# Six feature tiles transposed in place, and the PSUM banks of the last stage divided three and five

## The chip, the cores and the metric

The kernel runs on one core of one Trainium2 chip. The metric is the device time of one execution in microseconds (us). A core has five engines with an instruction stream each: TensorE (PE, matmul; its weight loads are listed as PEld), VectorE (DVE), ScalarE (ACT), GpSimd (POOL) and SyncE (SP). In this kernel SP issues most DMA transfers and POOL the rest. Each engine executes its stream in order and waits for others by semaphores.

## The reference

Two mixers read one layer norm of the same input, and their results are added to it.

```python
xn = layernorm(x)                                  # x: 1 x 2048 x 512
# A: linear attention, 32 heads of 16, learned softmax features
q, k, v = split_heads(xn @ wqkv)
pq, pk = q @ w_phi, k @ w_phi                      # per head
phi_q = concat(softmax(pq), softmax(-pq))          # phi_k alike, 32 features a head
kv, z = phi_k^T v, sum_s phi_k
o = (phi_q @ kv) / (phi_q . z + 1e-6)
A = merge_heads(o) @ wo                            # 512 x 512
# B: gated MLP with a spatial matmul
h = gelu(xn @ w_in)                                # 2048 x 1376
z1, z2 = h[:, :688], layernorm(h[:, 688:])
g = w_sp @ z2 + b_sp                               # w_sp: 2048 x 2048
B = (z1 * g) @ w_out                               # 688 x 512
out = x + A + B
```

All is float32, to float32 accuracy.

## The kernel before

The 2048 rows are 16 tiles of 128, numbered `s` or `i` from 0 to 15. For accuracy a matmul operand is split into a rounded part `h` (type float32r) and a rest `l`, and one product becomes three matmuls, `h*h`, `h*l` and `l*h` (`mm3`, lines 55 to 57). The first stages project, build the key sums and run the spatial matmul as seven block products per pair of tiles (`products`, `drain`). The unnormalised query features of each tile go to DRAM as `e_d`, and the gated rows `u = z1 * g` as `u_d` and `uT_d`.

This case is about the last stage, which for each pair of tiles (i, i+1) does on PE, in this order:

- `attend_T(i)`: 16 transposes of 128x128 of the pair's query features into four PSUM tiles (`ptq`). ACT copies them out as `f` (line 900).
- `project_u(i)`: 17 matmuls of 512 columns, u times w_out, into the PSUM tile `pout`.
- `attend`: 32 small matmuls (line 912) of `f` with the key-value sums `kvT` into two PSUM tiles `po`. ACT rounds each into `oT` high (line 47), DVE computes the rest (line 51).
- `project_u(i+1)`, 17 matmuls into a second `pout`.
- `project_o` for both tiles: 12 matmuls each, oT times wo, added into the same two `pout`. DVE then adds x (line 944, tile `xr`), and SP stores the result (line 945, `out<-xr`).

Beside this the features of later tiles are made ready (`features(s)`, three tiles ahead): SP loads `et` from `e_d` (line 487), DVE runs seven operations on it (`q_fin`, lines 494 to 501; line 501 writes the finished tile), and POOL issues a DMA that copies `et` into `er` (line 872). That copy gives the tile the type float32r, and the transposes read `er` at line 898. A tile without copy is read at line 896 as float32. Tiles 0 and 1 come from DRAM as float32r, and tiles 2 and 3 have no copy, so 12 tiles have one. The gated rows of later tiles are loaded as `ut`, joined by ACT (line 774) and split by ACT and DVE into `uh`, `ul` and `rt`.

PSUM has eight banks, and each of these tiles fills one. Before, `pst` holds four for `ptq`, and `pso` two for `pout` and two for `po`. A PSUM tile's next use waits until its last reader is done: a `pout` bank is free when DVE has added x from it. The last stage takes over banks in which the seven products of the stage before still stand until `drain` (lines 712 to 717) has read them.

One more piece of the stage before ends here: the gate of the last pair of rows (`gate`, from line 727) is issued in the round i = 8 and needs `z1t`, which `load_z1` fetches with a memset and two DMAs on POOL.

The scheduler orders each engine's stream when the program is built, from its own estimates; `tc.issue_after` pins a few places.

Of the kernel before, what the change touches and what calls it, by code (L numbers as in the profile page):

```python
# [10 lines left out]
F32 = mybir.dt.float32  # L11
# [8 lines left out]
P = 128  # L20
S, D, H, DH, FH = 2048, 512, 32, 16, 688
# [12 lines left out]
NP = NT // 2  # L34
# [5 lines left out]
def mixer(ctx: ExitStack, tc: tile.TileContext, x, x_t, wv, wqkT, phi_bd, wo, w_in, wst, b_r, w_out, out):  # L40
    nc = tc.nc
    pe, act, dve, pool, sp = nc.tensor, nc.scalar, nc.vector, nc.gpsimd, nc.sync


    def round_h(eng, h, src):
        if eng is act:
            return act.activation(h, src, AF.Copy).ins  # L47
        return eng.tensor_copy(h, src).ins

    def rest_l(l, src, h, eng=None):  # L50
        return (eng or dve).tensor_tensor(l, src, h.bitcast(F32), op=ALU.subtract).ins  # L51

    def mm3(dst, a, b, start, stop):
        (ah, al), (bh, bl) = a, b
        pe.matmul(dst, ah, bh, start=start, stop=False)  # L55
        pe.matmul(dst, ah, bl, start=False, stop=False)  # L56
        return pe.matmul(dst, al, bh, start=False, stop=stop).ins  # L57

    def pool_of(name, bufs, side=None, space=None):
        kw = {"space": space} if space else {"side": side}  # L60
        return tc.tile_pool(name=name, bufs=bufs, reuse_waits="tile", **kw)
# [3 lines left out]
    psum = lambda name, bufs: pool_of(name, bufs, space=PSUM)  # L65
# [424 lines left out]
    def q_fin(et, tmp, zb):  # L490

        e, r, t, w = et[:, :NF], *(et[:, NF + k * 2 * H:NF + (k + 1) * 2 * H] for k in range(3))
        den = et[:, NF + 6 * H:QW]
        dve.tensor_tensor(tmp, e, zb, op=ALU.mult)
        dve.tensor_reduce(t, heads(tmp), axis=AX.X, op=ALU.add)
        dve.tensor_tensor(t, t, r, op=ALU.mult)
        dve.scalar_tensor_tensor(den, pairs(t, 0), EPS_DEN, pairs(t, 1), op0=ALU.add, op1=ALU.add)
        dve.reciprocal(den, den)
        dve.tensor_tensor(w.rearrange("p (h a) -> p h a", a=2), r.rearrange("p (h a) -> p h a", a=2),
                          den.unsqueeze(2).to_broadcast([P, H, 2]), op=ALU.mult)  # L500
        return e, dve.tensor_tensor(heads(e), heads(e), bc(w, 2 * H), op=ALU.mult).ins
# [46 lines left out]
    with ExitStack() as p1:  # L548
# [41 lines left out]
        for s in range(NE):  # L590
            et = load_q(s, tb.tile([P, QW], F32, tag="et", bufs=2, name="et"))
            tmp = zw.tile([P, 4, FC], F32, tag="z2", bufs=2, name="qtmp").rearrange("p a b -> p (a b)")[:, :NF]
            e, _ = q_fin(et, tmp, zb)
# [56 lines left out]
    for s in range(NT):  # L650
# [4 lines left out]
        z = z2[n][:, 2 * (s % 2):2 * (s % 2) + 2]  # L655
# [34 lines left out]
    def load_z1(i):  # L690
        t = gt.tile([P, 2, UP], F32, tag="z1", name="z1t")
        pool.memset(t[:, :, FH + REM:], 0.0)
        for k in range(2):
            pool.dma_start(t[:, k, :FH], z1_d[2 * i + k])
        return t
# [46 lines left out]
    def slot(name, dt=F32):  # L742
        return xz.tile([P, 2, FH], dt, tag="xz", name=name).rearrange("p a b -> p (a b)")
# [8 lines left out]
    def split_w(t, h, l):  # L752
        return round_h(act, h, t), rest_l(l, t, h)
# [56 lines left out]
    g, es, ets = {}, {}, {}  # L810
    for n in range(NC):
        i = SEQ[n][0]
        if n % NQ == 1 and i < NP - 1:
            z = load_z1(i)
# [49 lines left out]
    def features(s):  # L864
        with tc.issue_after(fin[-1]):
            es[s], ins = q_fin(ets.pop(s), slot("qtmp")[:, :NF], zb)
        fin.append(ins)
        if s == 3:
            return
        e = es[s]  # L870
        es[s] = cw.tile([P, NF], F32R, tag="er", bufs=5, name="er")
        pool.dma_start(es[s].bitcast(F32), e)

    def gated(t):
        u = joined(t, cw.tile([P, UP], F32, tag="uj", bufs=2, name="uj"))
        return gate_parts(u, wk.tile([P, KF * P], F32R, tag="uh", name="uh"),
                          wk.tile([P, KF * P], F32R, tag="ul", name="ul"), wk.tile([2 * REM, P], F32R, tag="rt", name="rt"))
# [3 lines left out]
    ctx_psg.__exit__(None, None, None)  # L881
    fin.append(last)
    sp.dma_start(kvT.rearrange("p j b -> p (j b)"), kvT_d)
    pst = ctx.enter_context(psum("pst", 4))
    pso = ctx.enter_context(psum("pso", 1))

    def attend_T(s):

        fs = []
        for g in range(NG):  # L890
            pt = pst.tile([P, 2, 2, P], F32, tag="tr", name="ptq")
            for a in range(2):
                for k in range(2):
                    src = group(es[s + k], 2 * g + a)
                    if src.dtype == F32:
                        pe.transpose(pt[:, a, k], src, ident)
                    else:
                        pe.transpose(pt[:, a, k].bitcast(F32R), src, ident_r)  # L898
            f = wk.tile([P, 2, 2 * P], F32, tag="f", bufs=NG + 1, name="f")
            attend_T.last = act.activation(f, pt.rearrange("p a k b -> p a (k b)"), AF.Copy).ins  # L900
            fs.append(f)
        return fs

    def attend(fs):

        oT = [wk.tile([P, NG, 2 * P], F32R, tag=f"oT{k}", name="oT") for k in "hl"]
        po = [pso.tile([P, 2, 2 * P], F32, tag="po", bufs=2, name="po") for _ in range(2)]
        for j in range(2 * NG):
            c = j % NG
            for r in range(2):  # L910
                rows = slice(r * HP, (r + 1) * HP)
                lasts[3] = pe.matmul(po[r][c * QP:(c + 1) * QP, j // NG], kvT[rows, j], fs[j // 2][rows, j % 2],
                                     start=True, stop=True).ins
        for k in range(2):
            gs = slice(2 * k, 2 * k + 2)
            lasts[5] = round_h(act, oT[0][:, gs], po[k])
            ins = rest_l(oT[1][:, gs], po[k], oT[0][:, gs])
        return oT, ins

    def project_u(i, u, between=None):  # L920
        uh, ul, rt = u
        parts = [(slice(0, D), pso.tile([P, D], F32, tag="out", bufs=2, name="pout"))]
        if i == NT - 1:
            more = pst.tile([P, 4, P], F32, tag="tr", name="pout2").rearrange("p a b -> p (a b)")
            parts = [(slice(k * D // 2, (k + 1) * D // 2), q[:, :D // 2]) for k, q in enumerate((parts[0][1], more))]
        order = ExitStack()
        for ds, p in parts:
            for c in range(KF):
                i_ = mm3(p, (uh[:, c], ul[:, c]), tuple(w[:, ds] for w in wu[c]), c == 0, False)
                if between and c == KF // 2:  # L930
                    order.enter_context(between(i_))
            for w in wu[KF]:
                lasts[2] = pe.matmul(p, rt, w[:, ds], start=False, stop=False).ins
        order.close()
        return parts

    def project_o(i, oT, parts):
        ts = slice(i % 2 * P, (i % 2 + 1) * P)
        xr = wk.tile([P, D], F32, tag="xr", bufs=3, name="xr")
        sp.dma_start(xr, x[i * P:(i + 1) * P, :])  # L940
        for ds, p in parts:
            for c in range(ND):
                lasts[4] = mm3(p, (oT[0][:, c, ts], oT[1][:, c, ts]), (wo_h[:, c, ds], wo_l[:, c, ds]), False, c == ND - 1)
            dve.tensor_tensor(xr[:, ds], p, xr[:, ds], op=ALU.add)
            sp.dma_start(out[i * P:(i + 1) * P, ds], xr[:, ds])

    GATE_LAST = 8

    wo_h, wo_l = (cw.tile([P, ND, D], F32R, name=f"wo{k}") for k in "hl")
    p = {0: project_u(0, uT.pop(0))}  # L950
# [4 lines left out]
    with tc.issue_after(attend_T.last):  # L955
        for c in range(ND // 2, ND):
            wo_last, _ = split_w(wo_raw[c], wo_h[:, c], wo_l[:, c])
# [13 lines left out]
    def ahead(i):  # L971

        if 3 < i + 3 < NT:
            features(i + 3)
        if i + 4 < NT:
            ets[i + 4] = load_q(i + 4, slot("et"))
            us[i + 4] = fetch_u(i + 4)

    nxt = {}
    for i in range(0, NT, 2):  # L980
        if i:
            p[i] = project_u(i, nxt.pop(i))
            with tc.issue_after(lasts[2]):
                oT, _ = attend(fT)
            with tc.issue_after(lasts[3]):
                p[i + 1] = project_u(i + 1, nxt.pop(i + 1))
        if i + 2 < NT:
            with tc.issue_after(lasts[5]), tc.issue_after(wo_last):
                nxt[i + 2], nxt[i + 3] = gated(us.pop(i + 2)), gated(us.pop(i + 3))
        for k in range(2):  # L990
            project_o(i + k, oT, p.pop(i + k))
            ahead(i + k)
        if i == GATE_LAST - 4:
            z = load_z1(NP - 1)
        if i == GATE_LAST:
            with tc.issue_after(lasts[0]), tc.issue_after(lasts[1]):
                gate(NP - 1, cb, z, gt.tile([P, 2 * UP], F32, tag="pl", name="pl"))
            p2.close()
        if i + 2 < NT:
            with tc.issue_after(lasts[4]):  # L1000
                fT = attend_T(i + 2)
# [33 lines left out]
```

## Time and profile before

| | |
|---|---|
| time, 3 runs | 634.63 us median (634.57 to 634.85) |
| the profiled execution | 635.8 us, of which 634.1 us are the span from its first to its last instruction |
| granted TensorE clock, mean | 0.997 |
| busy share of the span: PE, DVE, ACT, POOL | 98%, 80%, 50%, 19% |
| the last stage | 493.97 to 634.1 us, 140.1 us |

The times in the views are microseconds from the first instruction of the profiled execution. A row of the timeline has start, duration, engine, line, operation, result and operands, and, in brackets, how long the engine was idle before it and whose signal ended the wait. A PE row's duration reaches beyond the start of the next, since matmuls are pipelined: two starts give the pace. A row of the windows gives the busy time of PE, PEld, DVE, ACT and POOL in a stretch, then the granted clock, the share of the DMA engines' time and GB/s.

### The profile page before, as it was taken

To read this page: it belongs to the slowest core of one execution; us is meant where nothing else is said; L and a number is where in the kernel's file an instruction comes from. 1 tells how busy PE (TensorE), PEld (TensorE's weight loads), DVE (VectorE), ACT (ScalarE), POOL (GpSimd) and SP (SyncE) were. 2 spreads that over 40 slices of the span, in tenths; PEclk is the share of its full clock that TensorE was granted. 3 is DMA by queue.
4 is the path that set the end of the run, shared out by engine and by line. 5 is a ranking of instruction groups with operands and counts; after the bars stand their busy time and mean duration, and the time that the engine had idled before them with its cause. 6 is when DMAs were issued, how large, how long until landed. Compare 5 with 4: busy or idle time off the path is not lost.

```text
span 634.1 us, 11506 instructions
## 1 busy us (share of the span) xinstructions
PE 623.6 (98%) x4375; PEld 563.9 (89%) x4375; DVE 507.1 (80%) x925; ACT 314.5 (50%) x463; POOL 122.3 (19%) x215
## 2 busy tenths in 40 slices
PE   8999999999999999999999999999999998998997
PEld 6888888888888999999999999999999876777776
DVE  5979989998898579889968777688686897999621
ACT  5623333332433447887465444654448552556650
POOL 4542231322101006442011010110103000000100
PEclk9999999999999999999999999999999998999999
DMA  8467676656644941002486776768677968598811
GB/s 329 150 167 161 188 185 147 194 141 155 178 141 108 296 159 67 2 1 68 145 224 173 212 196 177 227 184 228 188 231 255 314 230 279 198 229 307 249 66 36
DMA packets 67379, 113.90 MB, mean 180 GB/s; under 512 B 30620, under 2 KB 32156, under 8 KB 67324
## 3 DMA queue, kind: packets, MB, share of 16 engines
q1 hardware_dynamic: 53036, 63.35, 34.2%
q0 software_dynamic: 11696, 43.65, 24.2%
q10 hardware_dynamic: 2592, 6.16, 2.6%
q8 instruction: 34, 0.56, 0.4%
q14 instruction: 21, 0.17, 0.1%
HBM read 60.69 MB, written 31.48 MB: 145 GB/s over the span
## 4 chain that ended last, share of the span: by engine, by line
PE 82%; DMA 8%; DVE 6%; ACT 2%; issue 2%; SPq 0%; POOL 0%; ACTq 0%; DVEq 0%; POOLq 0%
PE g L57 10%; PE g L56 10%; PE g L55 10%; PE proj L55 6%; PE zps L55 6%; PE proj L57 6%; PE proj L56 6%; PE zps L57 6%; PE zps L56 6%; PE pout L55 3%; PE pout L56 3%; PE pout L57 3%; DMA et<-e_d 2%; DMA eq<-e_d 2%; PE kvps L322 1%
## 5 line engine op out<-in xcount | busy, mean ns | idle before, releaser
L55 PE MATMUL g<-B,A 128*128 128x344 f32 x448 | 143.2, 320 | 0.0
L56 PE MATMUL g<-B,A 128*128 128x344 f32 x448 | 143.2, 320 | 0.0
L57 PE MATMUL g<-B,A 128*128 128x344 f32 x448 | 142.9, 320 | 0.0
L55 PEld LDWEIGHTS g<-B,A 128*128 128x128 f32 x448 | 84.2, 188 | 0.0
L56 PEld LDWEIGHTS g<-B,A 128*128 128x128 f32 x448 | 84.2, 188 | 0.0
L57 PEld LDWEIGHTS g<-B,A 128*128 128x128 f32 x448 | 84.1, 188 | 0.0
L47 ACT ACTIVATE A<-S 128x512 fp32r<-128x512 f32 x64 | 39.7, 629 | 53.7 <-DVE S L538 23.3
L116 ACT ACTIVATE e<-e,r_x 128x1024 f32<-128x1024 f32 x32 | 36.7, 1149 | 46.0 <-DVE e L115 44.2
L51 DVE TENSOR_TENSOR A<-S,A 128x512 fp32r<-128x512 f32 x64 | 43.4, 688 | 17.0 <-ACT A L47 16.7
L55 PE MATMUL proj<-wqk_h,xT 128*128 128x512 f32 x124 | 49.6, 400 | 0.0
L57 PE MATMUL proj<-wqk_h,xT 128*128 128x512 f32 x124 | 48.8, 394 | 0.0
L56 PE MATMUL proj<-wqk_l,xT 128*128 128x512 f32 x124 | 48.7, 393 | 0.0
L118 DVE TENSOR_REDUCE sm<-e 128x64 f32<-128x1024 f32 x32 | 38.6, 1212 | 9.7 <-ACT e L116 9.4
L47 ACT ACTIVATE A<-wf 128x512 fp32r<-128x512 f32 x64 | 33.2, 518 | 26.4 <-PE g L57 20.6
L51 DVE TENSOR_TENSOR A<-wf,A 128x512 fp32r<-128x512 f32 x64 | 35.4, 553 | 9.9 <-ACT A L47 9.5
L55 PE MATMUL zps<-w_h,xT 128*128 128x344 f32 x128 | 41.8, 326 | 0.4 <-ACT z1f L146 0.3
L57 PE MATMUL zps<-w_h,xT 128*128 128x344 f32 x128 | 40.9, 319 | 0.0
L56 PE MATMUL zps<-w_l,xT 128*128 128x344 f32 x128 | 40.8, 319 | 0.0
L146 ACT ACTIVATE z1f<-zps,r_x 128x344 f32<-128x344 f32 (+1 forms) x30 | 17.0, 566 | 33.8 <-PE zps L57 33.3
L302 ACT ACTIVATE v<-proj,r_x 128x512 f32<-128x512 f32 x16 | 11.0, 687 | 44.2 <-PE proj L57 41.7
L55 PE MATMUL pout<-wu,uh 128*128 128x512 f32 (+1 forms) x75 | 30.2, 402 | 2.3 <-DVE rh L734 1.8
L900 ACT ACTIVATE f<-ptq 128x512 f32<-128x512 f32 x32 | 16.5, 601 | 29.4 <-PE ptq L898 23.2
(199 smaller groups left out, 1534.8 us busy)
## 6 DMA issues: line engine op xcount, KB each, us to landing
wf<-in_wst SPq DMA_DIRECT2D x64, 256.0 KB, 3.7
e_d<-e POOLq DMA_DIRECT2D x16, 544.0 KB, 3.7
et<-e_d SPq DMA_DIRECT2D x16, 544.0 KB, 5.1
zacc<-e POOLq DMA_DIRECT2D x16, 512.0 KB, 4.9
er<-et POOLq DMA_DIRECT2D x12, 512.0 KB, 5.3
z_d<-z1f ACTq DMA_DIRECT2D x16, 344.0 KB, 3.8
z1t<-z_d POOLq DMA_DIRECT2D x16, 344.0 KB, 5.7
u_d<-c POOLq DMA_DIRECT2D x14, 384.0 KB, 2.7
```

The costliest lines, as they stand in the source:

```text
L47: return act.activation(h, src, AF.Copy).ins
L51: return (eng or dve).tensor_tensor(l, src, h.bitcast(F32), op=ALU.subtract).ins
L55: pe.matmul(dst, ah, bh, start=start, stop=False)
L56: pe.matmul(dst, ah, bl, start=False, stop=False)
L57: return pe.matmul(dst, al, bh, start=False, stop=stop).ins
L116: softmax_pair.exp = act.activation(e, e, AF.Exp, scale=scale).ins
L118: dve.tensor_reduce(sm, heads(e), axis=AX.X, op=ALU.add)
L146: z1_raw.last = act.activation(z[:, k], p, AF.Copy, scale=r_x[:, s:s + 1]).ins
L302: ins = act.activation(v[s], proj(s, wv_h, wv_l, rest_last), AF.Copy, scale=r_x[:, s:s + 1]).ins
L322: ins = pe.matmul(kv_acc[k:k + QP, m // 4], vs[:, m * QP:(m + 1) * QP], e[:, m * HP:(m + 1) * HP], start=s == 0 and m < 4, stop=s == NT - ...
L900: attend_T.last = act.activation(f, pt.rearrange("p a k b -> p a (k b)"), AF.Copy).ins
```

## The change

Three things change. Features of tiles below `PLAIN = 6` get no copy, so tiles 4 and 5 lose theirs and their transposes read float32. The PSUM pools become five banks for `ptq`, `po` and the odd tile `pout2`, and three for `pout`. And `load_z1(NP - 1)` has to follow the last copy issued before it.

```diff
     def features(s):
...
         fin.append(ins)
-        if s == 3:
+        if s < PLAIN:
             return
         e = es[s]
         es[s] = cw.tile([P, NF], F32R, tag="er", bufs=5, name="er")
-        pool.dma_start(es[s].bitcast(F32), e)
+        features.copied = pool.dma_start(es[s].bitcast(F32), e).ins
...
-    pst = ctx.enter_context(psum("pst", 4))
-    pso = ctx.enter_context(psum("pso", 1))
+    pst = ctx.enter_context(psum("pst", 5))
+    pso = ctx.enter_context(psum("pso", 3))
...
     def attend(fs):
...
-        po = [pso.tile([P, 2, 2 * P], F32, tag="po", bufs=2, name="po") for _ in range(2)]
+        po = [pst.tile([P, 2, 2 * P], F32, tag="tr", name="po") for _ in range(2)]
...
     def project_u(i, u, between=None):
         uh, ul, rt = u
-        parts = [(slice(0, D), pso.tile([P, D], F32, tag="out", bufs=2, name="pout"))]
+        parts = [(slice(0, D), pso.tile([P, D], F32, tag="out", name="pout"))]
...
-    GATE_LAST = 8
+    GATE_LAST, PLAIN = 8, 6
...
         if i == GATE_LAST - 4:
-            z = load_z1(NP - 1)
+            with tc.issue_after(features.copied):
+                z = load_z1(NP - 1)
```

The first place is PE at the transposes of tiles 4 and 5, with - for before and + for the change. `zb` is the slot that holds the float32r identity, `ident` the float32 one.

```order
 L56 MATMUL pout<-wol,oT 128x512
 L57 MATMUL pout<-woh,oT 128x512
-L898 MATMUL ptq<-zb,er 128x128 x16
+L896 MATMUL ptq<-ident,et 128x128 x16
 L55 MATMUL pout<-wu,uh 128x512
 L56 MATMUL pout<-wu,uh 128x512
```

Nothing moved here: the 16 transposes keep their place and read `et`, the tile that DVE writes.

The second place is SP late in the stage, around the load of the last feature tile, number 15 (the first `et` row after the + line), the stores of output tiles 8 and 9 (`out<-xr`) and the loads of x.

```order
 L756 DMA_TRANSPOSE ut<-u_d 128x12x128
+L945 DMA out<-xr 128x512 x2
 L487 DMA et<-e_d 128x1088
-L945 DMA out<-xr 128x512 x2
 L940 DMA xr<-in_x 128x512 x2
 L756 DMA_TRANSPOSE ut<-u_d 128x12x128 x2
```

The load of tile 15 now stands behind the two stores, which wait for DVE's additions; before it stood ahead of them.

The third place is DVE in the same round, where it works on tile 15 (lines 494 and 495) and on the rests of `oT` for the pair (10, 11). Before:

```order
L494 TENSOR_TENSOR qtmp<-et,zb 128x1024
L495 TENSOR_REDUCE et<-qtmp 128x64
L51 TENSOR_TENSOR oT<-po,oT 128x512
L496 TENSOR_TENSOR et<-et 128x64
L51 TENSOR_TENSOR oT<-po,oT 128x512
```

And in the change:

```order
L494 TENSOR_TENSOR qtmp<-et,zb 128x1024
L51 TENSOR_TENSOR oT<-po,oT 128x512 x2
L495 TENSOR_REDUCE et<-qtmp 128x64
L51 TENSOR_TENSOR ul<-uj,uh 128x640
L496 TENSOR_TENSOR et<-et 128x64
```

Both rests moved up by one or two rows, and line 494 of tile 15, the first to need its load, stands ahead of them in both programs.

On POOL the memset and the two loads of `z1t` stand behind the third remaining copy, that of tile 8; before they stood ahead of all copies.

## The prediction

> **What bounds the kernel now.** I read the page first, then windows cut at the start of each pair's transposes in the last stage, then PE's timeline there.
>
> ```profile
> span 634.1 us, 11506 instructions
> PE 623.6 (98%) x4375; PEld 563.9 (89%) x4375; DVE 507.1 (80%) x925; ACT 314.5 (50%) x463; POOL 122.3 (19%) x215
> ```
>
> PE is busy for 623.6 of 634.1 us, so only its gaps and its slow stretches are to be had. The windows show where these lie; the first is pair (0, 1), and so on to (14, 15):
>
> ```profile
> 493.97:510.28 16.31, 16.31 (x109) 12.69 (x108) 13.95 (x22) 10.33 (x16) 0.00 (x0) 1.00 0.92 289
> 510.28:527.85 17.57, 17.34 (x108) 13.22 (x106) 16.89 (x26) 8.39 (x12) 1.07 (x2) 1.00 0.74 250
> 527.85:548.06 20.21, 17.65 (x108) 13.87 (x107) 14.93 (x26) 8.39 (x12) 1.06 (x2) 0.92 0.70 240
> 548.06:564.50 16.44, 16.12 (x107) 12.69 (x106) 14.95 (x23) 8.39 (x12) 1.59 (x3) 1.00 0.81 233
> 564.50:580.48 15.98, 15.98 (x107) 12.65 (x106) 14.97 (x26) 9.65 (x13) 1.06 (x2) 1.00 1.11 307
> 580.48:598.39 17.91, 16.14 (x108) 12.71 (x106) 15.21 (x26) 11.26 (x14) 2.69 (x5) 1.00 0.73 232
> 598.39:614.33 15.94, 15.94 (x107) 12.64 (x106) 4.32 (x6) 8.38 (x12) 0.00 (x0) 1.00 0.25 78
> 614.33:634.10 19.77, 16.39 (x136) 14.12 (x134) 3.52 (x6) 3.15 (x6) 0.00 (x0) 1.00 0.18 62
> ```
>
> An undisturbed pair takes 15.94 us, as (12, 13) does with PE busy throughout. Pair (4, 5) takes 20.21 and (10, 11) 17.91. The four PE gaps behind this are:
>
> ```profile
> 511.11 0.47 PE L55 MATMUL pout<-wu,uh 128*128 128x512 f32 x1 [0.23 <-DVE et L499]
> 530.87 1.45 PE L898 MATMUL ptq<-zb,er 128*128 128x128 f32 x12 [2.56 <-DMA er<-et]
> 549.85 0.47 PE L55 MATMUL pout<-wu,uh 128*128 128x512 f32 x1 [0.32 <-DVE xr L944]
> 583.73 0.47 PE L55 MATMUL pout<-wu,uh 128*128 128x512 f32 x1 [1.77 <-DVE rh L734]
> ```
>
> The largest waits for a copy into `er`. The other three stand at the first matmul of an even tile, which in the program waits for the addition that frees its `pout` bank; DVE's operation named in a bracket stands beside that addition.
>
> **Tiles 4 and 5 without copies.** Tile 5 was finished and copied so:
>
> ```profile
> 522.54 1.23 DVE L501 TENSOR_TENSOR et<-et 128x1024 f32<-128x1024 f32 x1
> 524.62 0.54 POOL L872 DMA_DIRECT2D er<-et  x1 [5.82 <-DVE et L501]
> 524.82 1.56 DVE L51 TENSOR_TENSOR ul<-uj,uh 128x640 fp32r<-128x640 f32 x2
> 532.00:534.00 2.00, 2.00 (x8) 1.61 (x7) 1.86 (x5) 1.42 (x3) 0.53 (x1) 0.50 0.86 249
> 534.00:536.00 2.00, 2.00 (x8) 1.63 (x7) 0.49 (x2) 0.00 (x0) 0.00 (x0) 0.76 0.91 301
> ```
>
> DVE was done at 522.54 + 1.23 = 523.77, four microseconds before PE's transposes began at 527.85; the copy landed only at 530.87. Without it the 2.56 us go. Nothing else is late there: `ul` of tiles 4 and 5, the next thing that PE needs, was ready at 526.38. The copies' own work goes with them, two issues on POOL and 1 MB on the DMA queues. The two windows add a second loss: the granted clock was 0.50 and 0.76 for four microseconds behind the wait. So the whole excess over an undisturbed pair is to be had, 20.21 - 15.94 = 4.27 us: 2.56 of waiting and 1.71 of slow clock and restart.
>
> [...]
>
> Against it stands the slower kind of transpose:
>
> ```profile
> 510.28 0.60 PE L896 MATMUL ptq<-ident,et 128*128 128x128 f32 x4
> 515.12 1.47 PE L896 MATMUL ptq<-ident,et 128*128 128x128 f32 x12
> 598.39 1.48 PE L898 MATMUL ptq<-zb,er 128*128 128x128 f32 x16
> ```
>
> Eight more float32 ones take 1.47 - 0.60 = 0.87, so sixteen take 1.47 + 0.44 = 1.91 against 1.48: 0.43 us more. Net: 4.27 - 0.43 = **3.84 us saved**.
>
> **Three banks for `pout`.** Tile i then waits for the addition of tile i-3, not i-2. For an even tile that addition belongs to the pair before the last, so the gaps 0.23, 0.32 and 1.77 go; for an odd tile it lies over four microseconds back (17 matmuls and the attend step come first). By the windows (6, 7) has 16.44 - 15.94 = 0.50 and (10, 11) 1.97 to spare, by the gaps alone 0.32 and 1.77; I take the middles, 0.41 and 1.87. With 0.23: **2.51 us saved**.
>
> **Five banks for `ptq` and `po`.** A pair needs six tiles, so the second `po` takes the bank of the pair's first `ptq`, which is free once ACT has copied the first `f`. The first `po` matmul reads that same `f`, so it waits for it anyway: nothing. Only with (2, 3), where `po` follows the transposes at once, has this no room, and there too the operand comes first.
>
> **The start of the stage.** In the built program the first `pout` was in the bank of product P7; now it is in that of P4, the last one that `drain` reads.
>
> ```profile
> 493.97 0.39 PE L55 MATMUL pout<-wu,uh_ul 128*128 128x512 f32 x1
> 494.17 0.58 DVE L712 SCALAR_TENSOR_TENSOR c<-g,bias,c 128x344 f32<-128x344 f32 x1 [0.31 <-PE g L57]
> 582.90 0.68 DVE L944 TENSOR_TENSOR xr<-pout,xr 128x512 f32<-128x512 f32 x1
> ```
>
> P4 is read until 494.17 + 0.58 = 494.75. The hand-over to PE took 583.73 - 583.58 = 0.15 at the 1.77 us gap. So the first matmul starts at 494.90, not 493.97: a **new wait of 0.93 us**. All behind it shifts, DVE too, whose `oT` hangs on PE.
>
> **`z1t` later.** The loads move behind the third copy, to about 546:
>
> ```profile
> 489.57 1.13 POOL L694 DMA_DIRECT2D z1t<-z_d  x2
> 577.36 1.34 ACT L729 ACTIVATE z1t<-z1t 128x1376 f32<-128x1376 f32 x1
> ```
>
> Their reader ran at 577.36 and comes some 4 us earlier: 25 us of cover. Their 0.69 MB replace the two lost copies' 1.05 MB in the stage: nothing.
>
> **The copy next in line.** Tile 7's copy is now the one closest to PE.
>
> ```profile
> 534.30 0.23 DVE L499 TENSOR_TENSOR et<-et 128x64 f32<-128x64 f32 x1
> 539.34 0.69 DVE L51 TENSOR_TENSOR oT<-po,oT 128x512 fp32r<-128x512 f32 x1 [4.81 <-ACT oT L47]
> DMA to landing us min/median/max: 2.9/5.3/9.7
> ```
>
> Before, line 501 of tile 7 stood behind an `oT` that waited 4.81 us; now it stands ahead of it. It ends at 534.53 + 0.7 (the shift) + 1.23 = 536.5, the copy is issued about 0.85 later (as for tile 5) at 537.3, and by the last row (the copies' issue to landing) it lands at 542.6, at the latest 547.0. PE needs it at 548.06 + 0.93 - 0.23 - 3.84 = 544.9. At the median nothing, at worst 2.1 us and another fall of the clock (1.7). I take nothing, the value at the median.
>
> **The load of tile 15.** SP now issues it behind the stores of tiles 8 and 9, and DVE's rests of `oT` for (10, 11) stand behind the operation that needs it.
>
> ```profile
> 576.24 0.53 SPq L487 DMA_DIRECT2D et<-e_d  x1
> 583.62 1.05 SPq L945 DMA_DIRECT2D out<-xr  x2
> 590.17 0.68 DVE L51 TENSOR_TENSOR oT<-po,oT 128x512 fp32r<-128x512 f32 x1
> 593.08 0.23 PE pout L55
> DMA to landing us min/median/max: 2.9/5.2/9.7
> ```
>
> The stores end their issue at 584.67. DVE reaches their additions about 4 us earlier, so the load goes out near 580.6, not at 576.24. PE's first `project_o` matmul of the pair (593.08) comes 5.4 us earlier, at 587.7, and needs the rest four matmuls (0.9) later, at 588.6. Line 494 (1.22) and one rest (0.68) come first, so the load must land by 586.7, within 6.1 us. The last row gives all `et` loads from 500 us on: median 5.2, nothing lost; longest 9.7, 3.6 lost. I take nothing, near the median, and keep 3.6 for the range. The loads of tiles 8, 12 and 13 stand ahead of an `oT` too, but moved behind no store; they go with the rival of late loads.
>
> **Sum.** 3.84 + 2.51 - 0.93 = 5.42 us. The profiled execution's 635.8 us (span 634.1, 1.7 around it) become 630.4. It lies 1.17 above the median of the runs, 634.63, from which the forecast is 634.63 - 5.42 = **629.2 us**.
>
> **Rivals.**
>
> *Loads late.* DVE meets a feature load that has not landed, in front of an `oT`, and PE waits. For it: DVE waited for such loads twice before,
>
> ```profile
> 560.73 1.23 DVE L494 TENSOR_TENSOR qtmp<-et,zb 128x1024 f32<-128x1024 f32 x1 [1.18 <-DMA et<-e_d]
> 573.31 1.23 DVE L494 TENSOR_TENSOR qtmp<-et,zb 128x1024 f32<-128x1024 f32 x1 [0.63 <-DMA et<-e_d]
> ```
>
> and it is busy for 15 of a pair's 16 us. Against it: the medians. Price 1 to 3.6, middle 2: 631.2 us.
>
> *The wait moves to pair (6, 7).* The removed wait returns at tile 7's copy: up to 2.1 + 1.7 lost, 633.0 us. Against it: the two removed copies, and the DMA engines' share of 0.12 just where this one runs:
>
> ```profile
> 538.00:540.00 2.00, 2.00 (x30) 1.37 (x15) 0.66 (x2) 1.29 (x3) 0.00 (x0) 1.00 0.12 38
> ```
>
> *The change does not bite.* If the wait at (4, 5) was for the features and not for their copy, only the banks remain: -2.51 + 0.93 + 0.43, so 633.5 us. Against it: line 501 ends four microseconds ahead.
>
> *Slower.* Six tiles in five rotating banks make PE pause in each pair, and the clock falls each time. Place: the first `po` of a pair. Price: 1.71 us a pair, as at (4, 5), in up to seven pairs, 12: 641 us. It decides from four pairs, where 6.8 exceed the gain of 5.42 by more than 1.3. Against it: six rotating banks left the clock at 1.00 in seven of the eight pairs, and `po` waits for no one new. [...]
>
> **How the numbers follow.** Forecast 0.70, from 628.3 (the first wait hidden) to 630.2 (up to 1 us of new waits). Loads late 0.17. Wait at (6, 7) 0.05. No bite 0.04. Slower 0.04. The range 628.0 to 632.2 holds the forecast and most of the late loads, and leaves out the last three. 0.2% is 1.3 us, about what a measurement of this kernel can tell from no change. Faster by more: 0.90, with all of the first two and most of the third. Within: 0.06, mostly no bite and the worst of the late loads. Slower: 0.04.
>
> **What would show it.** Right: pair (4, 5) near 16.4 us with clock 1.00 throughout, no gap at the first matmul of an even tile, a gap of 0.9 us at the first `pout`. Wrong: a gap at line 898 in (6, 7), or PE waiting for `oT` of (10, 11) with DVE's line 494 waiting for `et` ahead of it, or a clock below 1.00 in pairs that had none.

## The result, and the profile after

The change takes 629.96 us (median of 4 runs, 629.45 to 630.19) beside 634.6 us (632.66 to 634.85) of the kernel before. The ratio is 0.9932, with a 95% interval of 0.9912 to 0.9953. The forecast was 629.2 us, with a range of 628.0 to 632.2. Two further sets of runs of the change (below) gave 629.70 and 629.89 us, at ratios of 0.9915 (0.9885 to 0.9946) and 0.9918 (0.9889 to 0.9946).

The profiled execution took 630.09 us. Its page begins:

```profile
span 628.4 us, 11487 instructions
PE 622.3 (99%) x4375; PEld 563.1 (90%) x4375; DVE 505.3 (80%) x925; ACT 313.5 (50%) x463; POOL 121.0 (19%) x213
```

The span is 5.7 us shorter, and PE's busy time only 1.3 us: most of what went was waiting. The windows of the last stage, cut as before at the start of each pair's transposes (the columns are those of the table in the prediction):

```profile
495.26:511.36 16.10, 16.09 (x107) 12.67 (x107) 13.45 (x22) 10.58 (x16) 0.00 (x0) 1.00 0.75 240
511.36:528.47 17.11, 17.11 (x107) 13.19 (x106) 16.75 (x26) 8.39 (x12) 0.00 (x0) 1.00 0.61 207
528.47:544.79 16.32, 16.32 (x108) 13.01 (x107) 14.97 (x26) 8.39 (x12) 1.13 (x3) 1.00 0.85 276
544.79:560.75 15.96, 15.96 (x108) 12.64 (x106) 14.89 (x23) 8.39 (x12) 2.83 (x6) 1.00 0.94 264
560.75:576.72 15.97, 15.97 (x108) 12.63 (x107) 13.99 (x22) 9.64 (x13) 1.06 (x2) 1.00 0.91 297
576.72:592.68 15.96, 15.96 (x108) 12.64 (x106) 15.57 (x29) 11.26 (x14) 2.15 (x4) 1.00 0.84 265
592.68:608.64 15.96, 15.96 (x107) 12.64 (x106) 4.52 (x7) 8.38 (x12) 0.54 (x1) 1.00 0.32 106
608.64:628.40 19.76, 16.39 (x136) 14.12 (x134) 3.52 (x6) 3.15 (x6) 0.00 (x0) 1.00 0.20 62
```

In the first seven rows the length and PE's busy time, the first and second number, now agree to 0.01 us, and the granted clock is 1.00 in all of them. Pair (4, 5), the third row, fell from 20.21 to 16.32 us, (10, 11) from 17.91 to 15.96. What is left to be waited for stands at the start, in PE's timeline:

```profile
494.18 0.32 PE L57 MATMUL g<-B,A 128*128 128x344 f32 x1
495.26 0.47 PE L55 MATMUL pout<-wu,uh_ul 128*128 128x512 f32 x1 [0.76 <-DVE c L712]
```

The start of the first `pout` is 495.26 - 494.18 = 1.08 us after that of the last matmul of the stage before, where it was 0.16 us (493.81 to 493.97). These 0.92 us are the wait for the last operation of `drain`, the one that reads P4 (line 712 is a helper that four of its operations share). DVE's timeline:

```profile
494.54 0.58 DVE L712 SCALAR_TENSOR_TENSOR c<-g,bias,c 128x344 f32<-128x344 f32 x1 [0.31 <-PE g L57]
```

It ends at 494.54 + 0.58 = 495.12, and PE starts 0.14 us later. The view of the waits has no other line for PE from 470 us on (in total, times, longest):

```profile
PE pout L55 <- DVE c L712: 0.8, 1, 0.8
```

Three of the four gaps of before stood at a `pout` and the largest at `er`; all four are gone, and this one is new.

### The profile page after: what moved, and what is told of

The parts are those of the page before. It is cut to its first block, busy times and chain, and to the rows that moved or that the text cites. A ratio compares the mean times of both kernels' runs of the same rounds, so it can differ in the third digit from the quotient of the medians.

```text
span 628.4 us, 11487 instructions
## 1 busy us (share of the span) xinstructions
PE 622.3 (99%) x4375; PEld 563.1 (90%) x4375; DVE 505.3 (80%) x925; ACT 313.5 (50%) x463; POOL 121.0 (19%) x213
## 4 chain that ended last, share of the span: by engine, by line
PE 96%; DVE 3%; issue 0%; ACT 0%
PE g L57 11%; PE g L56 11%; PE g L55 11%; PE proj L55 6%; PE zps L55 6%; PE proj L57 6%; PE proj L56 6%; PE zps L57 6%; PE zps L56 6%; PE pout L55 6%; PE pout L56 5%; PE pout L57 5%; PE po L912 1%; PE kvps L322 1%; PE ptq L898 1%; PE pout L933 1%
## 5 line engine op out<-in xcount | busy, mean ns | idle before, releaser
L537 DVE TENSOR_TENSOR S<-wf 128x256 f32<-128x256 f32 x32 | 13.4, 420 | 27.1 <-DMA wf<-in_wst 27.1
```

Of the source, the lines that this page charges most:

```text
L537: dve.tensor_tensor(sums[:, 0], b[:, 0], b[:, 1], op=ALU.add)
```

## The experiments

Each kernel is a variant of the change unless it says otherwise. The lengths of the pairs in the profiled execution of each, from one start of the transposes to the next (for the first pair from the first `pout`), with the time from the last matmul of the stage before to the first `pout` ahead:

| kernel | first `pout` | (0,1) | (2,3) | (4,5) | (6,7) | (8,9) | (10,11) | span |
|---|---|---|---|---|---|---|---|---|
| before | 0.16 | 16.31 | 17.57 | 20.21 | 16.44 | 15.98 | 17.91 | 634.1 |
| before again | 0.16 | 16.02 | 17.44 | 17.80 | 16.42 | 15.97 | 17.51 | 630.6 |
| the change | 1.08 | 16.10 | 17.11 | 16.32 | 15.96 | 15.97 | 15.96 | 628.4 |
| the change again | 1.08 | 16.08 | 17.12 | 16.31 | 15.96 | 15.97 | 16.53 | 628.5 |
| banks alone | 1.08 | 16.09 | 17.13 | 16.91 | 16.00 | 15.98 | 15.95 | 628.6 |
| banks alone, order held | 1.08 | 16.10 | 17.12 | 19.52 | 16.01 | 15.98 | 15.96 | 631.3 |
| copies alone | 0.16 | 16.02 | 17.43 | 16.31 | 16.23 | 15.96 | 17.53 | 628.9 |
| first bank | 0.15 | 16.02 | 17.12 | 16.32 | 15.96 | 15.97 | 15.96 | 626.5 |
| eight plain | 1.08 | 16.09 | 17.13 | 16.31 | 16.31 | 20.72 | 15.97 | 633.7 |

### The banks alone

Tiles 4 and 5 get their copies back, the pools stay as in the change.

```diff
-    GATE_LAST, PLAIN = 8, 6
+    GATE_LAST, PLAIN = 8, 4
```

> The new PSUM division with the copies of tiles 4 and 5 put back. Theory (the copy's landing is what pair (4, 5) waited for, and the clock fell because of that wait): PE waits again about 2.5 us at line 898 of pair (4, 5), the granted clock falls below 0.8 for some 4 us behind it, the pair takes 19.8 to 20.3 us instead of 16.3, and the time is 633.4 to 634.0 us. Rival (the third pout bank and the DVE order that came with it had already cleared this wait, so the copies cost nothing): the pair stays at or below 16.4 us and the time is 629.5 to 630.2 us.

Measured: 631.53 us median (630.28 to 634.77, 8 runs), ratio 0.9944 (0.9914 to 0.9973), span 628.6. The median lies between the ranges of the theory and of the rival. The profiled execution was the fastest of the eight, and its span is far less than the terms of the prediction leave without the copies (-2.51 + 0.93, a span of 632.5). PE's timeline at pair (4, 5) says why:

```profile
528.00 0.45 PE L898 MATMUL ptq<-zb,er 128*128 128x128 f32 x4
528.29 0.47 PE L55 MATMUL pout<-wu,uh 128*128 128x512 f32 x1
...
532.30 1.15 PE L898 MATMUL ptq<-zb,er 128*128 128x128 f32 x12
533.39 2.08 PE L912 MATMUL po<-f,kvT 64*32 64x256 f32 x32
```

Four transposes run, then the 17 matmuls of `project_u(4)`, which need no copy, and only then the other twelve. By 532.30 the copy of tile 5 had landed, and PE did not wait for it in this execution. The price is that `attend` follows the transposes at once: its 32 matmuls take 2.08 us instead of the 1.09 of the kernel before. With two banks for `pout` the built program had all sixteen transposes ahead. So undoing one edit let the scheduler build another order, and this run does not measure the copies.

### The banks alone, with the order held

To measure them, `project_u(4)` is held behind the sixteenth transpose, as it stands in the kernel before (`attend_T.pe` keeps the last transpose). PE's stream differs from that of the banks alone in this place only; on DVE two neighbours change places.

```diff
-    GATE_LAST, PLAIN = 8, 6
+    GATE_LAST, PLAIN = 8, 4
...
-            p[i] = project_u(i, nxt.pop(i))
+            with tc.issue_after(attend_T.pe if i == 4 else lasts[4]):
+                p[i] = project_u(i, nxt.pop(i))
```

> The new PSUM division with the copies of tiles 4 and 5 (as in e1), and the 16 transposes of pair (4, 5) held ahead of project_u of tile 4, where the change has them. Theory now (the copy's landing is what was waited for; in e1 the scheduler used the earlier free pout bank to run project_u first and so hid it): PE waits 2 to 5 us at line 898 of pair (4, 5), as long as the copy of tile 5 takes beyond the arrival of PE, the granted clock falls behind it, the pair takes 19 to 23 us, and the time is 633 to 637 us. Rival (with three pout banks the features or the copy come early enough, whatever the order): no wait above 0.5 us and 629.5 to 631 us.

Measured: 633.38 us (631.21 to 634.81, 10 runs), ratio 0.9974 (0.9950 to 0.9999), span 631.3. The wait is back, at the same place as before the change:

```profile
528.16 0.46 PE L898 MATMUL ptq<-zb,er 128*128 128x128 f32 x4
530.56 1.59 PE L898 MATMUL ptq<-zb,er 128*128 128x128 f32 x12 [1.95 <-DMA er<-et]
531.96 0.76 PE L55 MATMUL pout<-wu,uh 128*128 128x512 f32 x1
532.51 0.63 PE L56 MATMUL pout<-wu,uh 128*128 128x512 f32 x1
```

The matmul started at 532.51 takes 0.63 us, where 0.39 is usual, and the windows show the clock, the seventh number, falling from 1.00 to 0.50:

```profile
527.51:530.92 3.41, 1.46 (x12) 1.15 (x11) 3.27 (x8) 0.00 (x0) 0.00 (x0) 1.00 0.92 326
530.92:534.34 3.42, 3.42 (x17) 2.94 (x16) 3.28 (x6) 2.06 (x4) 0.53 (x1) 0.50 0.86 268
```

Pair (4, 5) takes 19.52 us against 16.32 in the change, so with this order the lost copies are worth 3.20 us in this execution, and 3.68 us in the medians of the two kernels measured side by side (633.38 against 629.70). The other pairs agree with the change to 0.05 us. The mean granted clock was 0.997 or less in eight of these ten runs, and in none of the 18 runs of the change.

### The copies alone

The kernel before with tiles 4 and 5 plain, and `z1t` held as in the change; the pools stay as they were.

```diff
-    GATE_LAST = 8
+    GATE_LAST, PLAIN = 8, 6
...
-        if s == 3:
+        if s < PLAIN:
...
-        pool.dma_start(es[s].bitcast(F32), e)
+        features.copied = pool.dma_start(es[s].bitcast(F32), e).ins
...
-            z = load_z1(NP - 1)
+            with tc.issue_after(features.copied):
+                z = load_z1(NP - 1)
```

> The copies of tiles 4 and 5 left out, with the PSUM division of before. Theory (the gaps at even tiles are waits for a pout bank): pair (4, 5) takes about 16.4 us, gaps at the first matmul of tiles 2, 6 and 10 come back with about 0.2, 0.3 and 1.8 us, the first pout of the stage has no gap, and the time is 631.3 to 632.2 us. Rival (the gaps came from where the slow pair (4, 5) had put DVE, and go with it): no gap above 0.2 us at tiles 6 and 10, and without the first wait the time is 628.8 to 629.5 us.

Measured: 630.76 us (630.32 to 631.83, 6 runs), ratio 0.9919 (0.9891 to 0.9947), span 628.9. PE's timeline shows one wait of PE above 0.1 us left in the stage, at the first matmul of tile 10:

```profile
578.54 0.47 PE L55 MATMUL pout<-wu,uh 128*128 128x512 f32 x1 [1.38 <-DVE rh L734]
```

Pair (4, 5) is as short as in the change. Of the three gaps expected, only that at tile 10 came back, with 1.38 us instead of 1.8; at tiles 2 and 6 it is less than 0.1 us. The time lies between the range of the theory and that of the rival, so both have a part. What the banks add to the copies is read off the table: (2, 3) 0.32, (6, 7) 0.27 and (10, 11) 1.57 us less, the first `pout` 0.92 us more and (0, 1) 0.08 more, together 1.16 us less.

In the profiled executions each edit alone brings the span near 629, the two together to 628.4: either one takes the wait at (4, 5) away, one by having no copy, the other by another order on PE. The medians lie further apart. Measured side by side with these two kernels, the next one, the change with its pools swapped, took 628.47 us; with the 0.92 us of the first `pout` the change would have taken about 629.4 there, an estimate, the copies alone 1.4 and the banks alone 2.1 us more. One of the eight runs of the banks alone had a clock of 0.997 and took 634.77 us, which suggests that the other order does not always cover the copy; no profile shows that run.

### The first bank

The new wait at the first `pout` comes from which bank it gets. Opening the pool of three first puts it into the bank of product P2, which `drain` reads earlier; every engine's order stays the same.

```diff
-    pst = ctx.enter_context(psum("pst", 5))
     pso = ctx.enter_context(psum("pso", 3))
+    pst = ctx.enter_context(psum("pst", 5))
```

> The change with the two PSUM pools opened in the other order, so that the first pout stands in the bank of product P2, which is read early, and each engine's stream is the same as in the change. Theory (the 0.76 us gap at the first pout is the wait for the bank of P4): the gap goes, the first pout follows the last product's matmul within 0.2 us, all behind it comes 0.9 us earlier, and the time is 628.8 to 629.4 us. Rival (the next thing is as late: the rest of u or the transposes' banks): the same 0.5 to 0.9 us show up as a gap within the first pair, and the time is 629.8 to 630.1 us.

Measured: 628.47 us (628.22 to 630.12, 6 runs), ratio 0.9886 (0.9856 to 0.9916), span 626.5. PE's timeline there:

```profile
493.30 0.32 PE L57 MATMUL g<-B,A 128*128 128x344 f32 x1
493.45 0.39 PE L55 MATMUL pout<-wu,uh_ul 128*128 128x512 f32 x1
```

The gap is gone, and PE waits nowhere in the last stage. The median is a little below the range expected. The span is 1.9 us shorter than that of the change because this execution also reached the stage 0.88 us earlier (493.30 against 494.18); that belongs to the execution, since in the second profile of the same kernel it is 493.93. For a direct comparison it ran once more beside the change:

> The kernel with the two pool lines swapped once more, beside the change in the same call, for a direct comparison. Theory (the first bank costs 0.76 to 0.93 us and nothing else differs): no wait of PE at the first pout, span 626.5 to 627.3, median 628.3 to 629.0, under the change by 0.8 to 1.3 us in this call. Rival (the earlier 628.47 owed something to its call): median within 0.4 us of the change's.

> The change once more, as the companion of the swapped lines. Theory: 629.7 to 630.1 median, wait of 0.76 us at the first pout, granted clock not below 0.999 in any run, spread under 1 us. Rival (the narrow spread was luck): some runs with the clock at 0.997 or less and 2 us and more above the fastest.

Measured: 628.92 us (628.50 to 630.18, 6 runs), ratio 0.9907 (0.9874 to 0.9940), beside 629.89 (629.39 to 630.38, 8 runs) for the change. The difference of 0.97 us agrees with the 0.92 read off the profile. Five of its six runs lie below the fastest of the change. This kernel is faster than both.

### Eight plain tiles

If plain features are good for tiles 4 and 5, tiles 6 and 7 could have them too.

```diff
-    GATE_LAST, PLAIN = 8, 6
+    GATE_LAST, PLAIN = 8, 8
```

> The change with PLAIN at 8, so that tiles 6 and 7 have no copy either. Theory (where no copy is waited for, the float32 transposes are all that is paid): pair (6, 7) takes 16.3 to 16.4 us instead of 15.96, all other pairs stay within 0.1, and the time is 630.2 to 630.6 us. Rival 1 (leaving a copy out helps in itself, by less DMA traffic and earlier feature loads): 629.5 us or less. Rival 2 (the feature slots, held until PE has read them, delay the loads of later tiles): DVE waits more than 1 us longer for et and the time is above 630.9 us.

Measured: 631.94 us (630.07 to 638.95, 10 runs), ratio 0.9958 (0.9925 to 0.9992). The profiled execution took 635.45 us. It is one of three of the ten with a clock of 0.997 or less (635.45 to 638.95 us); the other seven took 630.07 to 632.58. It shows the rival of the late loads at work, in the timelines of SP, DVE and PE:

```profile
563.35 0.43 SPq L487 DMA_DIRECT2D et<-e_d  x1
573.92 1.23 DVE L494 TENSOR_TENSOR qtmp<-et,zb 128x1024 f32<-128x1024 f32 x1 [4.42 <-DMA et<-e_d]
575.06 1.28 DVE L51 TENSOR_TENSOR oT<-po,oT 128x512 fp32r<-128x512 f32 x2
575.80 0.50 PE L57 MATMUL pout<-woh,oT 128*128 128x512 f32 x1 [2.85 <-DVE oT L51]
```

The load, that of tile 13, was issued at 563.35 and its reader started at 573.92, over ten microseconds later. The issue is only 1.0 us later than in the change (562.34), so slots held for longer can account for 1.0 us at most. The two rests of `oT` stood behind that reader on DVE, PE waited 2.85 us for them, and then the clock fell. In the change one of the two rests stands ahead of the reader: here too the edit changed the built order, and what each of the two did was not tried apart. Pair (8, 9) took 20.72 us instead of 15.97. Pair (6, 7) shows the price of sixteen float32 transposes where no wait goes with the copy: 16.31 us against 15.96. PE had not waited for the copies of tiles 6 and 7, and taking them away is a loss of some 2 us (631.94 against 629.70 to 629.96 for the change).

### The third edit undone

```diff
-            with tc.issue_after(features.copied):
-                z = load_z1(NP - 1)
+            z = load_z1(NP - 1)
```

> The change without its third edit: the loads of z1t stay ahead of the copies on POOL, and run near 490 us. Theory (they are covered by some 25 us in either place): the same pairs within 0.1 us, 629.5 to 630.3 us. Rival 1 (near 546 us they delay feature loads): DVE's waits for et become shorter by 1 us or more. Rival 2 (near 490 us they delay the loads of wo and of the first features): PE or ACT waits 0.5 us or more longer near 500 us, and the time is 630.5 us or more.

Measured: 630.01 us (629.75 to 631.25, 8 runs), ratio 0.9927 (0.9901 to 0.9953), span 628.0. POOL's timeline of this kernel, and then that of the change:

```profile
490.75 0.57 POOL L694 DMA_DIRECT2D z1t<-z_d  x1
```

```profile
545.55 0.54 POOL L694 DMA_DIRECT2D z1t<-z_d  x1
```

The load moved by 55 us, and with it some of SP's loads of x and of features changed places. The time hardly moved: beside the change's 629.70 us, measured side by side, the ranges overlap, and the pairs agree with those of the change to 0.06 us, (0, 1) too, so nothing was lost near 500 us. DVE waited 2.0 us for feature loads, and between 2.4 and 4.0 us in the profiles of the change; if the earlier place makes these waits shorter, PE gained nothing from it.

### Both kernels again

> The change itself again, to have its spread beside that of the kernel before on one chip. Theory (the kernel before waits for a copy whose landing differs from run to run, and the change has no such wait on PE): the change spreads over less than 1.5 us, 629.3 to 630.8, where the kernel before spreads over 4 us and more. Rival (the feature loads in front of the rests of oT make the change depend on landings as much): a spread of 3 us or more, with runs above 632 us.

> The kernel before, for a second profile. Theory (its spread is the landing time of the copy of tile 5, and a wait there takes the clock down): PE waits at line 898 of pair (4, 5) again, between 1 and 6 us, the time over 628.5 us is about that wait plus 1.5 to 2 us for the clock plus some 2 us at even tiles. Rival (the spread comes from elsewhere, such as the start of the kernel): the wait is 2.4 to 2.7 us again, and another stretch makes the difference.

The change: 629.70 us (629.43 to 630.17, 6 runs), span 628.5, ratio as given above. Its profile has one more wait of PE than the first, in pair (10, 11), which takes 16.53 us instead of 15.96:

```profile
588.09 0.50 PE L57 MATMUL pout<-woh,oT 128*128 128x512 f32 x1 [0.27 <-DVE oT L51]
```

DVE had waited 2.69 us for the load of tile 12 at 567.01 and was 1.2 us later with the rests of `oT` (587.35 instead of 586.18). A third profile of the change has no such wait.

The kernel before: one run of 632.27 us, span 630.6, 3.5 us shorter than in its first profile. Most of the difference lies at one place, in PE's timeline:

```profile
527.18 0.46 PE L898 MATMUL ptq<-zb,er 128*128 128x128 f32 x4
529.27 1.22 PE L898 MATMUL ptq<-zb,er 128*128 128x128 f32 x12 [1.64 <-DMA er<-et]
530.32 0.47 PE L55 MATMUL pout<-wu,uh 128*128 128x512 f32 x1
```

The window of that pair, with the clock as the seventh number:

```profile
527.18:544.98 17.80, 16.16 (x108) 12.70 (x106) 14.95 (x26) 8.39 (x12) 1.05 (x2) 1.00 0.79 264
```

PE waited 0.92 us less for the copy than in the first profile (1.64 instead of 2.56), and the clock stayed at 1.00. The pair took 17.80 us instead of 20.21.

The runs without a trace agree. Beside these experiments the kernel before ran 57 times. In 32 of these runs the mean granted clock was 0.997 or less, and their median is 636.4 us; in the other 25 it was 0.999 or 1.000, and their median is 633.7. Of the 18 runs of the change, from 629.39 to 630.38 us, none had a clock below 0.999. These runs do not say where the clock fell. In the profiles it fell behind tile 5's copy: once in the kernel before (a wait of 2.56 us), and again with the order held (1.95 us), where the copies are back.

## Why the prediction was right, step by step

**What bounds the kernel.** PE did, and after the change it waits once in the stage (twice in the second profile).

**The copies, -3.84 us.** Pair (4, 5) went from 20.21 to 16.32, so -3.89. PE's timeline of the change:

```profile
528.47 1.91 PE L896 MATMUL ptq<-ident,et 128*128 128x128 f32 x16
```

The 1.91 us of the sixteen float32 transposes came as worked out, and the clock kept 1.00. That both losses go with the copies is shown by the order held, where the wait (1.95 us) and the fall of the clock (to 0.50) came back with them. The size of the term, however, belongs to one execution: before again would have given 17.80 - 16.32 = 1.48 us. The forecast took a wait with a fall of the clock as the usual one; 32 of the 57 runs have such a clock, little more than half.

**The third bank, -2.51 us.** (2, 3), (6, 7) and (10, 11) lost 0.46, 0.48 and 1.95 us, together 2.89. That is 0.38 us more than forecast, but not all of it is the banks' work. Beside the copies alone the banks bring 0.32 + 0.27 + 1.57 = 2.16 us at these three pairs, 0.35 less than the term. The other 0.73 us had gone without them, and before again is also shorter there (17.44, 16.42 and 17.51 us).

**Five shared banks, 0.** No wait of PE at `ptq` or `po` and no loss of clock: right. With six tiles through five banks PE was busy for all of the 15.96 us of pair (6, 7), at a clock of 1.00.

**The first `pout`, +0.93 us.** Measured 0.92, and the first bank's kernel confirms the cause: with every engine's order the same and only the bank another, the wait is gone.

**`z1t`, 0.** Right within 0.3 us, by the run with this edit undone (630.01 against 629.70).

**Tile 7's copy, 0 (at worst 3.8).** POOL's timeline of the change:

```profile
537.00 0.54 POOL L872 DMA_DIRECT2D er<-et  x1 [4.13 <-DVE et L501]
```

The issue was forecast for 537.3. PE did not wait for this copy in any of the three profiles.

**The load of tile 15, 0 (at worst 3.6).** SP's and DVE's timelines of the change:

```profile
579.21 0.42 SPq L487 DMA_DIRECT2D et<-e_d  x1
585.05 1.22 DVE L494 TENSOR_TENSOR qtmp<-et,zb 128x1024 f32<-128x1024 f32 x1
586.18 1.28 DVE L51 TENSOR_TENSOR oT<-po,oT 128x512 fp32r<-128x512 f32 x2
```

The load left 1.4 us before its forecast, the reader ran without a wait at 585.05, and the rests of `oT` followed in time. The prediction misread the row that gave it the longest landing, 9.7 us: that row is for the tile `et` and mixes the twelve loads with the twelve copies out of it. The loads alone (line 487 of the kernel before, from 495 us on; three landings are known) have

```profile
DMA to landing us min/median/max: 4.0/4.8/6.9
```

so no known load took 9.7 us, and the longest known would have lost 0.8 us instead of 3.6. Late loads did reach PE by another way: in the second profile of the change the load of tile 12 cost pair (10, 11) 0.57 us. DVE waited 2.4, 4.0 and 3.2 us for feature loads in the three profiles of the change, 1.8 and 0.6 in the two of before, so in these profiles the change has them closer to PE. The run with eight plain tiles shows them at 4.75 us (20.72 - 15.97), more than the price of 1 to 3.6 put on them.

**The sum.** -5.42 forecast, -5.70 measured in the span. Beside the terms above, pair (0, 1) was 0.21 us shorter and the stage began later by 0.37 us upstream (the last matmul ahead of it started at 494.18 instead of 493.81; in the second profile of before, at 493.56). Both were not forecast and lie within what executions of one program differ there: in the other two profiles of the change that matmul started at 493.71 and 494.48, and (0, 1) took 16.02 us in before again. That the two sums come so close is in part luck, since each rests on one execution: against before again the span is 2.2 us shorter (630.6 to 628.4), and the medians of the three sets of runs differ by 4.6 to 4.9 us.

**The median.** This step was wrong, by a small amount: the profiled execution lay 1.17 us above the median, and the forecast carried these 1.17 us over to the change. The change has no such distance (630.09 against 629.96). Of the 3.5 us between the two profiles of the kernel before, 2.41 lie at pair (4, 5), where the copy of tile 5 is waited for, and that goes with the change. That the other runs spread for the same reason is likely and not shown. Without the 1.17 the forecast would have been 630.4 us, 0.4 above the measured median instead of 0.8 below it.

**The rivals.** "Does not bite" fell with line 896 running without a wait. The wait at (6, 7) did not show in the three profiles of the change, and a slower clock in none of its 18 runs.

## What to carry to other kernels

A wait for a DMA that lands just too late can be worth more than the wait: here it was 2.56 us in one execution and 1.64 in another, and behind waits of 1.95, 2.56 and 2.85 us it also cost clock, so look for a clock below 1.00 in the windows after each wait of PE. When PSUM pools are divided anew, ask which old tile's bank the first new tile inherits and when its last reader is done; here the order of two lines was worth 1 us. An edit undone in a scheduled kernel can change the order of the rest, so hold the order before reading a cost off the difference.

## What the runs showed of the hardware

**The clock fell behind waits of 1.95, 2.56 and 2.85 us, each time to 0.50 and for 3.41 or 3.42 us.** Behind PE waits of 1.64 us (tile 5, before again) and 1.77 us (tile 10, before) the granted clock of the pair stayed at 1.00. It fell behind 1.95 us (order held, windows above), 2.56 us (before) and 2.85 us (eight plain). PE's busy time is the second number of the windows, the clock the seventh. The kernel with eight plain tiles, where the first row begins within the wait and the second is the stretch at 0.50:

```profile
573.91:577.32 3.41, 1.52 (x7) 1.26 (x8) 3.40 (x4) 1.63 (x3) 0.00 (x0) 1.00 1.06 284
577.32:580.73 3.41, 3.41 (x10) 2.67 (x9) 3.34 (x8) 0.00 (x0) 0.00 (x0) 0.50 0.80 243
```

The kernel before at pair (4, 5), from the end of the wait on:

```profile
530.87:531.54 0.67, 0.67 (x8) 0.67 (x8) 0.67 (x2) 0.19 (x1) 0.00 (x0) 1.00 0.85 268
531.54:534.96 3.42, 3.42 (x14) 2.84 (x13) 2.81 (x6) 1.88 (x4) 0.53 (x1) 0.50 0.89 289
534.96:535.60 0.64, 0.64 (x5) 0.51 (x4) 0.00 (x0) 0.00 (x0) 0.00 (x0) 1.00 0.94 302
```

PE had been running again for 1.5 us when the clock halved with eight plain tiles (575.80 to 577.32), for 0.7 us in before (530.87 to 531.54) and 0.4 with the order held (530.56 to 530.92). What the fall costs beyond the wait is 1.63 us with the order held (19.52 - 15.94 - 1.95), 1.71 in before (20.21 - 15.94 - 2.56) and 1.90 with eight plain tiles (20.72 - 15.97 - 2.85); without a fall the wait of 1.64 us cost only 0.22 beyond itself (17.80 - 15.94 - 1.64).

These are five waits in four executions, and no run varied the length of a wait alone. What decides whether the clock falls was not shown.

**One feature load took over ten microseconds.** The one of tile 13 with eight plain tiles needed 10.57 us from its issue (563.35) to its reader's start (573.92), and that of tile 12 in the three profiles of the change 8.2 to 9.4 us, where the landings known in before are 4.0 to 6.9 us. Over the pair in which the first of these was under way (561.37 to 582.09) the DMA engines moved 241 GB/s for it and for others; what held it up was not tried.
